# A planned decode kernel: nine transposing matmuls for sixteen, one projection for four batches, and new orders

## The chip, the cores and the metric

The kernel runs on one core of one Trainium2 chip. The metric is the device time of one execution in microseconds, the median of several runs. TensorE is PE in the profile (PEld its weight loads), VectorE DVE, ScalarE ACT, GpSimd POOL, and SyncE SP.

## The reference

Two layers of decoding for four batches, one token each, a model width D of 512. A layer is attention over a cache (32 query heads in 8 groups, 4096 keys, 128 elements a head) and a gated unit with 1792 hidden elements. Both layers use the same weights and the same cache.

```python
B, Sq, D = 4, 1, 512
Hq, Hkv, Sk, Dh = 32, 8, 4096, 128

def _A_ref(x, k_cache, v_cache, wq, wo):
    q = (x @ wq)                                   # per head, (B, Hq, 1, Dh)
    scores = einsum("bhqd,bhkd->bhqk", q, k) * (Dh ** -0.5)   # k, v repeated 4 times
    p = softmax(scores)
    o = einsum("bhqk,bhkd->bhqd", p, v)
    return o.reshape(B, Sq, Hq * Dh) @ wo

def _B_ref(x, w_gate, w_up, w_down):
    return (sigmoid(x @ w_gate) * (x @ w_up)) @ w_down

x = x + _A_ref(layernorm(x), K, V, wq, wo)
x = x + _B_ref(layernorm(x), w_gate, w_up, w_down)
x = x + _A_ref(layernorm(x), K, V, wq, wo)
x = x + _B_ref(layernorm(x), w_gate, w_up, w_down)
```

All inputs are bfloat16. K and V of one batch and one key-value head are 1 MB each.

## The kernel before

The work is cut into 64 units (layer, batch, key-value head), taken two at a time as 32 pairs. ORDER names the pairs: `013` is layer 0, batch 1, heads 6 and 7. Layer 1 of a batch can begin only when all four pairs of its layer 0, and then the gated unit and the new queries of that batch, are done, so pairs of both layers and of several batches are mixed.

K and V come from HBM into 12 slots of 1 MB; late in the kernel the four parts of the query weights' place become slots too. KEPT names the K and V that stay in their slot from layer 0 to layer 1; all others are loaded twice. LOADS is the order of all loads, one letter each (`k`, `v`, and `o`, `g`, `u`, `d` for the weights). One queue, SP's, issues them in that order. The function `pump` issues the next load as soon as a slot is free; the wait for the slot's last reader is a wait of SP, and everything behind it in LOADS waits too.

PROGRAM is the order of all steps, one letter each, in groups that begin where a pair's scores do. Each engine gets its share of the steps in this order and goes through them without overtaking. The letters, with the engine and the line that carries the work:

| letter | step | engine, line |
|---|---|---|
| `t`, `T` | half, or the whole, of a K tile transposed in 32 x 32 blocks | DVE L984 |
| `b` | the pair's query blocks | POOL L725 |
| `s`, `z` | first and second half of the pair's scores; `z` frees K slots | PE L1001 |
| `m`, `p`, `n` | row maxima, spread over the rows, made a bias | DVE L1019, PE L1024, DVE L1033 |
| `e` | Exp, with its sums | ACT L1044 |
| `P` | Exp transposed into the bank PT | PE L1063 |
| `C`, `D` | two halves of PT copied out as bfloat16, four copies each | ACT L1115 |
| `h`, `r`, `i` | sums split in two parts, summed per head, inverted | POOL L1074, PE L1129, DVE L1141 |
| `a` | half of one unit's product with V (PV); four to a pair, the second and fourth free a V slot | PE L1161 |
| `o` | `normalise`: the product times the inverted sums, into oT | DVE L1200 |
| `w`, `W` | `do_wo`: an out projection of units that are ready, added to x | PE L1219, DVE L1235 |
| `.` | one of 17 steps of a batch's gated unit and new queries | mostly PE L803, L828, L874, L923 |
| `x` | row sums of the out weights for the last unit | ACT L587 |

The buffer oT has two columns per head. Column 0 holds what is projected alone; column 1 holds a layer-1 result of batches 0 to 2 (`held`), which waits for a mate of another batch with the same unit, so that two columns go through the weights at once. `W` projects even where a mate would still come; a held result that is in the way of the next is flushed alone in `normalise`. A group for a pair of units is 32 matmuls.

After the last PV, `mean_of_last` (line 615) brings the mean of the last layernorm forward: it takes the last projection's part in it straight from oT. Then come layernorm, gated unit and the store for all four batches at once, with nothing left to load.

## Time and profile before

| | |
|---|---|
| median of 3 runs | 314.98 us (314.69 to 315.49) |
| the profiled execution | 316.39 us |
| its span, first to last instruction | 314.6 us |
| read from HBM | 119.80 MB |
| PE, DVE, ACT, POOL busy | 70%, 56%, 33%, 13% |
| PE matmuls, weight loads | 4826 each |

The page divides the span into 40 equal slices with one digit each for the busy share of an engine, the clock granted to PE and the DMA engines. Groups of instructions are by line; behind the bar stands the idle time of the engine before them and what ended it. In a timeline, the columns are start, duration, engine, line, operation, tiles, shapes, count, and in brackets the idle time before. A row of stretches has the busy time of each engine with its instructions, then the granted clock, the DMA share and the rate.

### The profile page before, as it was taken

What the parts mean: (1) busy time and instruction counts of PE and PEld (TensorE: products, weight loads), DVE (VectorE), ACT (ScalarE), POOL (GpSimd) and SP (SyncE); (2) the same over time, 40 slices, a digit from 0 to 9 for tenths busy, and PEclk for the clock granted to TensorE, in tenths of its full rate; (3) what the DMA queues carried; (4) which work ended last, traced back from release to release, by engine and by line L of the source; (5) the groups of instructions that cost most, each with busy time, mean ns of one, the idle gap of its engine ahead of it and who ended that gap; (6) DMA issues with size and microseconds to landing.
All of it is one profiled execution on the core that took longest, in us unless ns stands there. A gap on an engine that the chain in (4) does not pass through costs nothing.

```text
span 314.6 us, 11202 instructions
## 1 busy us (share of the span) xinstructions
PE 221.0 (70%) x4826; PEld 144.6 (46%) x4826; DVE 176.3 (56%) x410; ACT 104.8 (33%) x347; POOL 40.6 (13%) x205
## 2 busy tenths in 40 slices
PE   1233345327778768878988789877747888699796
PEld 1220223124555344647455646345543743455685
DVE  6266666324325657385951477865664797932243
ACT  2000322103303555342244534334333302366420
POOL 0011111100001203021021211021011110231000
PEclk9999999999985555565565557565555576555555
DMA  7999999999999999999999999999999899999900
GB/s 296 421 409 405 425 405 411 373 413 418 399 421 419 409 405 351 425 418 405 415 362 364 421 382 422 418 421 416 423 416 388 343 397 397 422 423 419 410 35 5
DMA packets 20792, 120.52 MB, mean 383 GB/s; under 512 B 1924, under 2 KB 6024, under 8 KB 7688
## 3 DMA queue, kind: packets, MB, share of 16 engines
q1 hardware_dynamic: 20720, 119.81, 94.3%
q8 instruction: 38, 0.62, 0.8%
q14 instruction: 10, 0.08, 0.1%
q10 hardware_dynamic: 24, 0.01, 0.0%
HBM read 119.80 MB, written 0.00 MB: 381 GB/s over the span
## 4 chain that ended last, share of the span: by engine, by line
PE 28%; DMA 13%; DVE 11%; ACT 6%; issue 5%; POOL 2%; DVEq 0%; ACTq 0%; POOLq 0%; SPq 0%
PE O_ps L1161 9%; PE S_ps L1001 9%; DVE slot L984 8%; DMA slot<-in_A_k_cache_dram 7%; DMA slot<-in_A_v_cache_dram 6%; ACT pT L1115 5%; PE PT L1063 2%; PE O_ps L1219 2%; POOL qz L725 1%; ACT pe L1044 1%; PE M_ps L923 1%; PE M_ps L874 1%; DVE small L1019 1%; PE S_ps L1443 1%; PE M_ps L738 1%
## 5 line engine op out<-in xcount | busy, mean ns | idle before, releaser
L984 DVE STREAM_TRANSPOSE slot<-slot 128x2048 f32<-128x2048 f32 (+1 forms) x53 | 103.9, 1973 | 17.4 <-DMA slot<-in_A_k_cache_dram 17.2
L1115 ACT ACTIVATE pT<-PT 32x128 bf16<-32x128 f32 x236 | 63.3, 268 | 90.7 <-PE PT L1063 64.3
L1001 PE MATMUL S_ps<-slot,qz 128*16 128x512 bf16 x512 | 60.4, 598 | 21.0 <-DVE slot L984 8.6
L1161 PE MATMUL O_ps<-pT,slot 128*128 128x4 bf16 x1696 | 54.2, 166 | 27.9 <-DMA slot<-in_A_v_cache_dram 18.2
L1161 PEld LDWEIGHTS O_ps<-pT,slot 128*128 128x128 bf16 x1696 | 50.8, 104 | 45.3 <-issue 15.9
L725 POOL COPY qz<-qs 32x32 bf16<-32x32 bf16 x128 | 26.1, 204 | 107.6 <-PE S_ps L1001 54.0
L1019 DVE TENSOR_REDUCE small<-S_ps 128x1 bf16<-128x512 f32 x32 | 21.9, 685 | 29.5 <-PE S_ps L1001 29.3
L1044 ACT ACTIVATE pe<-S_ps,small 128x512 bf16<-128x512 f32 x32 | 22.0, 687 | 44.4 <-DVE small L1033 34.9
L1001 PEld LDWEIGHTS S_ps<-slot,qz 128*16 128x16 bf16 x512 | 10.6, 101 | 36.6 <-issue 10.8
L1219 PE MATMUL O_ps<-oT,wo 128*128 128x2 bf16 (+1 forms) x672 | 21.6, 165 | 5.7 <-issue 3.9
L1219 PEld LDWEIGHTS O_ps<-oT,wo 128*128 128x128 bf16 x672 | 19.8, 104 | 9.2 <-issue 4.9
L1063 PE MATMUL PT<-ident_bf,pe 128*64 128x32 bf16 x512 | 19.2, 215 | 2.9 <-ACT pe L1044 2.0
L1063 PEld LDWEIGHTS PT<-ident_bf,pe 128*64 128x64 bf16 x512 | 15.8, 150 | 9.9 <-ACT pe L1044 4.9
L1074 POOL CAST small<-small 128x1 bf16<-128x1 f32 x32 | 6.0, 188 | 100.1 <-ACT pe L1044 80.9
L1200 DVE TENSOR_TENSOR oT<-O_ps,small 128x8 bf16<-128x8 f32 (+1 forms) x32 | 5.1, 160 | 22.0 <-PE O_ps L1161 14.4
L1235 DVE TENSOR_TENSOR small<-small,O_ps 128x4 f32<-128x4 f32 x34 | 4.0, 147 | 23.3 <-PE O_ps L1219 22.1
L1033 DVE CUSTOM_DVE_ANT_0 MS<-MS,small 128x64 f32<-128x64 f32 x32 | 9.2, 288 | 11.5 <-PE MS L1024 7.0
L874 PE MATMUL M_ps<-wq,small 128*1 128x512 bf16 x128 | 14.2, 608 | 0.0
L1024 PE MATMUL MS<-valid_p,small 128*128 128x64 bf16 x32 | 7.2, 224 | 6.9 <-DVE small L1019 6.7
L889 ACT ACTIVATE t_row<-M_ps,small 128x512 bf16<-128x512 f32 x4 | 2.7, 687 | 21.4 <-PE M_ps L874 17.7
L1129 PEld LDWEIGHTS O_ps<-small 128*128 128x128 bf16 x62 | 4.4, 111 | 10.4 <-issue 5.4
L1024 PEld LDWEIGHTS MS<-valid_p,small 128*128 128x128 bf16 x32 | 3.5, 109 | 12.5 <-DVE small L1019 11.2
(117 smaller groups left out, 187.0 us busy)
## 6 DMA issues: line engine op xcount, KB each, us to landing
slot<-in_A_v_cache_dram SPq DMA_DIRECT2D x49, 1024.0 KB, 10.8
slot<-in_A_k_cache_dram SPq DMA_DIRECT2D x45, 1024.0 KB, 11.6
wq<-in_A_v_cache_dram SPq DMA_DIRECT2D x6, 1024.0 KB, 12.6
wq<-in_A_wq_dram SPq DMA_DIRECT2D x2, 2048.0 KB, 10.2
wo<-in_A_wo_dram SPq DMA_DIRECT2D x8, 512.0 KB, 18.6
wg<-in_B_w_gate_dram SPq DMA_DIRECT2D x2, 896.0 KB, 17.5
wu<-in_B_w_up_dram SPq DMA_DIRECT2D x2, 896.0 KB, 20.1
wd<-in_B_w_down_dram SPq DMA_DIRECT2D x1, 1024.0 KB, 24.0
```

Of the source, the lines that this page charges most:

```text
L725: (lambda a, ps: lambda e: e.tensor_copy(qz_sb[ps, :, :, a, :], qs_sb[b][ps, :, u * REP:(u + 2) * REP].rearrange("p t (u r) -> p u t r", r ...
L874: (lambda k, st: lambda e: e.matmul(M_ps[h][32 * st:32 * st + 1, :], lhsT=xc_bf[:, k, 0:1], rhs=wv[:, k, h, :, st, :], start=(k == 0), sto ...
L984: dve(lambda e: e.transpose(kf, kf), writes=[f"s{st}"])
L1001: (lambda t, b2, e_, c, r0, ul: lambda e: e.matmul(S_ps[p][r0:r0 + 4 * REP, :], lhsT=qz_sb[:, ul, t, :, :].rearrange("p a r -> p (a r)"), ...
L1019: dve(lambda e: e.tensor_reduce(rm_bf, S_ps[p][:, :], AX.X, ALU.max), reads=[f"S{p}"], writes=["rmb"])
L1024: lambda e: e.matmul(MS[:, 0:16 * REP], lhsT=rm_bf.broadcast_to([P, P]), rhs=valid_p[:, :], start=True, stop=True),
L1033: lambda e: e.tensor_tensor_reduce(MS[:, 128:128 + 16 * REP], MS[:, 0:16 * REP], mask_f.rearrange("p n w -> p (n w)"), rowk_f, BIG, ALU.ad ...
L1044: lambda e: e.activation(pe_sb.rearrange("p j m -> p (j m)"), S_ps[p][:, :], ACTF.Exp, bias=nm_sb, scale=exp_scale, accum_out=sm_sb,),
L1063: (lambda x1, j, a1, n: lambda e: e.matmul(PT[64 * a1:64 * a1 + 64, n:n + 32], lhsT=pe_sb[:, j, 64 * x1:64 * x1 + 64], rhs=valid_bf[:, :, ...
L1115: (lambda dst, frm: lambda e: e.activation(dst, frm, ACTF.Copy))(dst, frm),
L1161: (lambda n, x, c, j: lambda e: e.matmul(bank[:, ul * REP:(ul + 1) * REP], lhsT=vv[:, x * JG + c * 4 + j, :], rhs=pT[:, x % 2, x // 2, j, ...
L1219: (lambda c, r: lambda e: e.matmul(O_ps[p][:, 64 + 2 * c:64 + 2 * c + nb], lhsT=wo_sb[:, us[0] * REP + r, cols(c)], rhs=oT_sb[:, us[0] * R ...
```

## The change

ORDER, LOADS and PROGRAM are replaced, with KEPT as it was. `ptrans` takes nine matmuls in place of 16: the four parts of the Exp tile are seen as one row of 512 columns, and a weight of 128 of them is taken every 64 columns, so that neighbours overlap; seven matmuls have 128 columns of weights and 64 result columns each, the two at the ends 64 and 32. `copies` and the PV read the new places. oT has one column per batch; in layer 1 a unit is projected once, when all four batches have their result there, with four columns. `held`, `mate_comes` and `W` are gone, `mean_of_last` has one set of eight matmuls for four columns, and x gets one addition per projection.

```diff
 
 KEPT = ["012345/23", "0145/45", "167/067", "014567/7"]
 ORDER = """
-003 002 000 001 013 011 101 010 012 100 102 022 021 020 023 112 110 031 103 111 123 032 030 033 120
-113 121 131 122 133 132 130
+000 003 002 001 013 011 101 010 012 102 100 021 022 020 023 112 110 111 031 113 123 030 032 033 120
+103 121 122 131 133 130 132
 """
 LOADS = """
-kkkkokovvk kkokvvkvoo kooovkvgvu guddvvvkkv kkvvkkvvvv kkvvkkvkvk vvvvvvkkvk kvvvkkvvkk vvkkvvkkvv
-kvvkkkvkkk vkkvvvvvvv vvvvv
+kkookkkook kovvokvvvo vokkvkkvgg uuddvvvkkv kkvvkkvvvv kkvvvkkvkk vvvvvvkkvk kvvvkkvvkk vvkkvvkkvv
+kvvkkkvkvk kkkvvvvvvv vvvvv
 """
 PROGRAM = """
-szmptntTeb shzPmDrpneTChiaawbT sazmbpTaTPonrD sTzCmpiaenahTbaaroiPDeC sazaaTamhPWprbnoiCTa
-sDaePzWhamawpoDnW.eC.rhP..iWr......aa.W..aaoi..CaDa.t.twbt szmtpnaebax
-shPzmrpCboiaDanaePThaoriCTDWWaax szWabmapntx sezPmhpWCrbtonx szDTiwbe
-szahamaPaopmCDrnWiaa.ap.enTahor..WPbT..ehiD szCaaa.aom..btWWrP.tipT..nDC.aaeT
-szh..PmawapnrCoe.iTWhDb.P saazbrmaaopn sizCaebw szmDhaaaPpornDCiehWaaamPapnrCoiDaeTWbaTwaahoPr.C
-szmDi.paaW.ne..bhTT.PaaWr s.zomC.pnib.a.Daa.eaTPT....DC sohrizm.aa.aabp snehztrmPCDoipnbeatTaP
-saazCohrimpDbnaaaTaePhDtoriCtaa szampnaoweTPhWribCaTDa szmaapnoePTWDbhri
-szCamWapnaeahPoCbritDWta.Ta..TW. sz..amab.pT.o.n s.zWmw.T.e...PChprni..aDbTawe szbTTmhPrwaaoC
-spznDiaeamPhpbrwaneaowi sCzhDbraaPm saapDzonCmweiPhpnCab
-saaaezrDoiPmhrpaaaanCeoDiWahaaaoPrCDiwaaNawWa
+szmpneTtthPrTib szDmptnetCb sazaaaPomCDbphTwwrnT seiaazPawhmbpranoDiCaehaPttaTa
+sroiwCawzDmpaTanebaTo shwPD.z.mr..pi.w.CneP...hr.aa...waaoi..CaDa..bTw swztmtpnebahaox
+sPCzmriwDpnTaebhaaaPorwiCTaDax szaawmpbwnx sztmtePbpx shDzrCwwnobetitwmaah
+spnzPawamoCrDpeihwa.a.ntaaPeD..Cbt.T.roiP szaam.haar.poi.C.anDaT.w.e.w.Thrb.aao szmPDTp.bnCeiwh.PaTa
+szambap szneroDmwpCb szniaahPrbameaowiCDharPapwanaCDoiTewaahTaaoP.ri szDmC.apban.wTe.T..hPraaoD
+s.iz.C.abm.a.panaTe.o.hPr.wTC. siD.za.amwpwaabwn soezthrmtpiPwnDCbeaaT
+shPaaCzmropinTaDeahaaPboCriDaTaw szmapneaTPChwoDriTbwaa szaampbnoTePhwrDi
+szCabmawwpnweaahPoritwtCa.DaT.T.. sz..maa.boTp.. s.zm.nbwT....pePhrtCnDi.aeat. shzPTraaTmCb
+sopnizDeawbmaPhwapwaonCDr szibemaaphnPC srzembaaD
+soiwPphCneaaraDawwoziwaPaamDaohrpiwCanaeaaPoChDwariaaNwa
 """
 
 
...
     t_row = sbt([P, D], dt.float32, "t_row")
     qs_sb = [sbt([P, NT4, HQ], dt.bfloat16, f"qs{b}") for b in range(Bn)]
     qz_sb = sbt([P, 2, NT4, 4, REP], dt.bfloat16, "qz")
-    oT_sb = sbt([P, HQ, 2], dt.bfloat16, "oT")
+    oT_sb = sbt([P, HQ, Bn], dt.bfloat16, "oT")
     pe_sb = sbt([P, 4, P], dt.bfloat16, "pe")
-    pT_sb = sbt([P, 2, 2, 4, 4, REP], dt.bfloat16, "pT")
-    NSMALL = 128
+    pT_sb = sbt([P, 2, 4, 2, 4, REP], dt.bfloat16, "pT")
+    NSMALL = 112
     small_sb = sbt([P, NSMALL], dt.float32, "small")
     used = [0]
 
...
             writes=["M1"],
         )
 
-    def mean_of_last(us, batches):
+    def mean_of_last(us):
         u = seq[NU - 1][2]
         assert us == [u]
-        cb = [(c, bb) for c, bb in enumerate(batches) if bb is not None]
         S.last_write["M1"] = S.group(
             "pe",
             [
-                (lambda n, r, c, bb, at_end: lambda e: e.matmul(
-                    M_ps[1][:, bb:bb + 1], lhsT=ws_hl[:, n, r:r + 1].broadcast_to([P, P]),
-                    rhs=oT_sb[:, u * REP + r, c:c + 1], start=False, stop=at_end,
-                ))(n, r, c, bb, (n, r, c) == (1, REP - 1, cb[-1][0]))
-                for c, bb in cb for n in range(2) for r in range(REP)
+                (lambda n, r: lambda e: e.matmul(
+                    M_ps[1][:, 0:Bn], lhsT=ws_hl[:, n, r:r + 1].broadcast_to([P, P]),
+                    rhs=oT_sb[:, u * REP + r, 0:Bn], start=False, stop=(n == 1 and r == REP - 1),
+                ))(n, r)
+                for n in range(2) for r in range(REP)
             ],
-            reads=["wsb"] + [f"oT_{u}_{c}" for c, _ in cb],
+            reads=["wsb"] + [f"oT_{u}_{c}" for c in range(Bn)],
         )
 
     def square_sums_of_parts():
...
 
     def ptrans(g):
         fns = []
-        for x1 in range(2):
-            for j in range(4):
-                for a1 in range(2):
-                    n = 32 * (4 * x1 + j)
-                    fns.append(
-                        (lambda x1, j, a1, n: lambda e: e.matmul(
-                            PT[64 * a1:64 * a1 + 64, n:n + 32],
-                            lhsT=pe_sb[:, j, 64 * x1:64 * x1 + 64],
-                            rhs=valid_bf[:, :, 8 * a1:8 * a1 + 8].rearrange("p g (a h) -> p a g h", a=2),
-                            start=True,
-                            stop=True,
-                        ))(x1, j, a1, n)
-                    )
+        pe_flat = pe_sb.rearrange("p j m -> p (j m)")
+        for q0, q1, c0, m0, m1 in (
+            [(64, P, 0, 0, 64)]
+            + [(0, P, 64 * w + 32, 64 * w, 64 * w + P) for w in range(7)]
+            + [(0, 64, 480, 448, 512)]
+        ):
+            a0, a1 = q0 // 32, q1 // 32
+            fns.append(
+                (lambda q0, q1, c0, m0, m1, a0, a1: lambda e: e.matmul(
+                    PT[q0:q1, c0:c0 + 16 * (a1 - a0)],
+                    lhsT=pe_flat[:, m0:m1],
+                    rhs=valid_bf[:, :, 4 * a0:4 * a1].rearrange("p g (a h) -> p a g h", h=REP),
+                    start=True,
+                    stop=True,
+                ))(q0, q1, c0, m0, m1, a0, a1)
+            )
         S.group("pe", fns, reads=["pe0"] + IDENT, writes=["PT"])
 
     def split_sums(g):
...
         n = buffer_of[g]
         if n == 0:
             return pT_sb, "pT0"
-        return slot[spare[0]][:, 0:16 * 4 * REP].rearrange("p (x y j g r) -> p x y j g r", x=2, y=2, j=4, g=4), "pT1"
+        return slot[spare[0]][:, 0:16 * 4 * REP].rearrange("p (x j y g r) -> p x j y g r", x=2, j=4, y=2, g=4), "pT1"
 
     def copies(g, x0):
         late = g == NP - 1
...
         for a in range(4):
             a1, a0 = divmod(a, 2)
             q = 64 * a1 + 32 * x0
-            dst = pT[32 * a:32 * a + 32, x0, :, :, :, :].rearrange("p x j g h -> p (x j) (g h)")
-            frm = PT[q:q + 32, 0:256].rearrange("p (n a w) -> p n a w", a=2, w=16)[:, :, a0, :]
+            dst = pT[32 * a:32 * a + 32, x0, :, :, :, :].rearrange("p j x g h -> p (j x) (g h)")
+            frm = PT[q:q + 32, :].rearrange("p (n a w) -> p n a w", a=4, w=16)[:, :, 2 * (1 - a1) + a0, :]
             if late and a1:
                 S.inst(
                     "dve",
...
                         (lambda n, x, c, j: lambda e: e.matmul(
                             bank[:, ul * REP:(ul + 1) * REP],
                             lhsT=vv[:, x * JG + c * 4 + j, :],
-                            rhs=pT[:, x % 2, x // 2, j, 2 * ul + c, :],
+                            rhs=pT[:, x % 2, j, x // 2, 2 * ul + c, :],
                             start=(n == 0 and c == 0 and j == 0),
                             stop=(n == XJ - 1 and c == 1 and j == 3),
                         ))(n, x, c, j)
...
         if part != 0 and (l == 1 or not kept("v", i)):
             free.append(where.pop(("v", b, u)))
 
-    held = {}
     ready = []
     done = set()
+    own_column = max((i, b) for i, (l, b, _) in enumerate(seq) if l == 0)[1]
 
     def normalise(g, uls=(0, 1)):
         l, b, u = seq[2 * g]
         bank, key = out_of(g, uls[0])
-        c = 1 if l == 1 and b < Bn - 1 else 0
+        c = b if l == 1 else own_column
         u0, n = u + uls[0], len(uls)
-        old = sorted({held[u + ul] for ul in uls if c and u + ul in held})
-        for bb in old:
-            us = [u + ul for ul in uls if held.get(u + ul) == bb]
-            for x in us:
-                held.pop(x)
-            wo_units(us, (None, bb), (g + 1) % 2)
         for ul in uls:
-            assert c or not any(t[2] == u + ul for t in ready)
+            assert not any(t[0] == l and t[2] == u + ul for t in ready)
             done.add((l, b, u + ul))
-            if c:
-                held[u + ul] = b
-            else:
+            if l == 0 or all((1, bb, u + ul) in done for bb in range(Bn)):
                 ready.append((l, b, u + ul))
         dve(
             lambda e: e.tensor_tensor(
...
             writes=[f"oT_{u + ul}_{c}" for ul in uls],
         )
 
-    def wo_units(us, batches, p, then=None):
-        c0 = 0 if batches[0] is not None else 1
-        cs = [c for c in range(2) if batches[c] is not None]
-        nb = len(cs)
+    def wo_units(us, l, b, p, then=None):
+        bs = range(Bn) if l == 1 else [b]
+        cs = range(Bn) if l == 1 else [own_column]
+        nb = len(bs)
         n = REP * len(us)
+        out_w = O_ps[p][:, 64:64 + KD * nb]
         fns = []
         for c in range(KD):
             for r in range(n):
                 fns.append(
                     (lambda c, r: lambda e: e.matmul(
-                        O_ps[p][:, 64 + 2 * c:64 + 2 * c + nb],
+                        out_w[:, c * nb:(c + 1) * nb],
                         lhsT=wo_sb[:, us[0] * REP + r, cols(c)],
-                        rhs=oT_sb[:, us[0] * REP + r, c0:c0 + nb],
+                        rhs=oT_sb[:, us[0] * REP + r, cs[0]:cs[0] + nb],
                         start=(r == 0),
                         stop=(r == n - 1),
                     ))(c, r)
...
             "pe", fns, reads=[f"oT_{u}_{c}" for u in us for c in cs] + [f"wo{u}" for u in us], writes=[f"O{p}"]
         )
         if then is not None:
-            then(us, batches)
-        for n_, c in enumerate(cs):
-            bb = batches[c]
-            dve(
-                (lambda n_, bb: lambda e: e.tensor_tensor(
-                    xT[:, :, bb],
-                    xT[:, :, bb],
-                    O_ps[p][:, 64:64 + 2 * KD].rearrange("p (k two) -> p k two", two=2)[:, :, n_],
-                    ALU.add,
-                ))(n_, bb),
-                reads=[f"x{bb}", f"O{p}"],
-                writes=[f"x{bb}"],
-            )
-
-    def mate_comes(t):
-        l, b, u = t
-        if u in held:
+            then(us)
+        dve(
+            lambda e: e.tensor_tensor(
+                xT[:, :, bs[0]:bs[0] + nb],
+                xT[:, :, bs[0]:bs[0] + nb],
+                out_w.rearrange("p (k b) -> p k b", k=KD),
+                ALU.add,
+            ),
+            reads=[f"O{p}"],
+            writes=[f"x{bb}" for bb in bs],
+        )
+
+    def do_wo(p, then=None):
+        if not ready:
             return False
-        end = 2 * last[l, b] if l == 0 else NU - 1
-        return any(pos[1, b2, u] <= end + 1 and (1, b2, u) not in done for b2 in range(Bn - 1))
-
-    def do_wo(p, force=False, then=None):
-        todo = [t for t in ready if force or not mate_comes(t)]
-        if not todo:
-            return False
-        l, b, u = todo[0]
+        l, b, u = ready.pop(0)
         us = [u]
-        if (l, b, u + 1) in todo and u % 2 == 0:
+        if u % 2 == 0 and (l, b, u + 1) in ready:
+            ready.remove((l, b, u + 1))
             us.append(u + 1)
-        for x in us:
-            ready.remove((l, b, x))
-        mates = {held.get(x) for x in us}
-        if len(mates) == 1 and None not in mates:
-            for x in us:
-                held.pop(x)
-            wo_units(us, (b, mates.pop()), p, then)
-        else:
-            wo_units(us, (b, None), p, then)
+        wo_units(us, l, b, p, then)
         return True
 
     ln_a(0, Bn, RS)
...
             k_turn(i)
         elif c == "x":
             wo_row_sums(sums_left.pop(0))
-        elif c in "wW":
-            do_wo((count["o"] + 1) % 2, c == "W")
+        elif c == "w":
+            do_wo((count["o"] + 1) % 2)
         elif c == ".":
             b, f = passes.pop(0)
             assert count["o"] > last[0, b] and not any(t[:2] == (0, b) for t in ready)
...
     assert all(count[c] == n for c, n in dict(D=NP, r=NP, i=NP, o=NP - 1, N=1, a=4 * NP).items())
     g = NP - 1
     xkeys = [f"x{b}" for b in range(Bn)]
-    while do_wo((g + 1) % 2, True):
+    while do_wo((g + 1) % 2):
         pass
     parts(sq_hl, xT.rearrange("p k b -> p (k b)"), xkeys, "rb")
     mean_before()
     normalise(g, (1,))
-    do_wo((g + 1) % 2, True, mean_of_last)
-    assert not ready and not held
+    do_wo((g + 1) % 2, mean_of_last)
+    assert not ready
     free += spare
     assert not loads and len(free) == NSLOT + KD
 
```

## The prediction

> **What bounds the kernel now.** I read the page first (totals, slices, the chain that ended last), then the answer by stretches, then the queue that issues the loads, and last the final microseconds one instruction at a time.
>
> ```profile
> span 314.6 us, 11202 instructions
> ...
> PE 221.0 (70%) x4826; PEld 144.6 (46%) x4826; DVE 176.3 (56%) x410; ACT 104.8 (33%) x347; POOL 40.6 (13%) x205
> ...
> PEclk9999999999985555565565557565555576555555
> DMA  7999999999999999999999999999999899999900
> GB/s 296 421 409 405 425 405 411 373 413 418 399 421 419 409 405 351 425 418 405 415 362 364 421 382 422 418 421 416 423 416 388 343 397 397 422 423 419 410 35 5
> ...
> HBM read 119.80 MB, written 0.00 MB: 381 GB/s over the span
> ...
> PE 28%; DMA 13%; DVE 11%; ACT 6%; issue 5%; POOL 2%; DVEq 0%; ACTq 0%; POOLq 0%; SPq 0%
> ...
> slot<-in_A_v_cache_dram SPq DMA_DIRECT2D x49, 1024.0 KB, 10.8
> ```
>
> The DMA row is full from the second slice to slice 38, and empty in the last two. At the 416 GB/s of an ordinary stretch (128 to 160 us in the next fence) the 119.80 MB take 288 us; the last two slices, in which nothing is left to load, are another 15 us. So about 12 us of the span are neither. The engines are not the bound by their totals (PE 70%), yet the chain puts 28% on PE and 13% on DMA: loads and compute hand over to each other, because a load may start only when a step of the program has given a slot back. The stretches tell where that hand-over fails:
>
> ```profile
> core 0: us, PE busy (x) PEld busy (x) DVE busy (x) ACT busy (x) POOL busy (x), PEclk, DMA share, GB/s
> ...
> 104.00:128.00 24.00, 18.58 (x362) 10.60 (x362) 15.41 (x30) 12.34 (x40) 5.19 (x26) 0.50 0.99 390
> 128.00:160.00 32.00, 26.97 (x606) 18.48 (x600) 22.26 (x54) 13.18 (x43) 4.47 (x22) 0.61 1.01 416
> 160.00:172.00 12.00, 11.33 (x238) 6.44 (x235) 2.64 (x12) 3.51 (x13) 2.02 (x10) 0.50 0.93 342
> ...
> 240.00:268.00 28.00, 23.75 (x437) 14.25 (x437) 21.53 (x50) 8.33 (x27) 3.25 (x16) 0.61 0.97 378
> ...
> 300.00:314.60 14.60, 11.07 (x368) 10.17 (x365) 6.13 (x36) 2.12 (x8) 0.00 (x0) 0.50 0.02 6
> ```
>
> Against 416 GB/s, 104 to 128 lacks 24 x 26/416 = 1.5 us of transfer, 160 to 172 lacks 12 x 74/416 = 2.1 us, and 240 to 268 lacks 28 x 38/416 = 2.6 us: 6.2 us in all. That is the most that new orders can win back inside the loads. The queue shows what a failing hand-over looks like:
>
> ```profile
> 103.87 1.99 SPq L366 DMA_DIRECT2D slot<-in_A_v_cache_dram  x2
> 110.31 1.81 SPq L366 DMA_DIRECT2D slot<-in_A_k_cache_dram  x2
> ...
> 151.70 14.84 SPq L366 DMA_DIRECT2D slot<-in_A_v_cache_dram  x6
> 166.59 3.14 SPq L366 DMA_DIRECT2D slot<-in_A_k_cache_dram  x2
> ```
>
> A load of 1024 KB takes 1.049 MB / 416 GB/s = 2.5 us of transfer. Between the end of the issues at 105.86 and the next at 110.31 lie 4.45 us, the time of 1.8 loads; and six V loads take from 151.70 to 166.54, 14.8 us where their transfer takes 15.1, so no reserve builds up ahead of 166. The order of the steps on PE decides there.
>
> **The change, part by part.** First the loads. I counted LOADS, ORDER, KEPT and NSLOT: 115 slot and weight loads after the query weights, the same sizes, the same number kept. So the transfer time stays. I then walked both PROGRAM strings and wrote down for every load which step frees its slot, with the PE work ahead of that step. From load 38 (counted from 0) on, 75 of the 77 positions wait for the same kind of step of the same pair; ahead of them stands the same PE work within 0.9 us, apart from one that is 2.1 us earlier. The big difference is the head: pair 000 comes first, and five output-weight loads stand before its second V load, where two stood. That load goes from 12.6 MB into the queue to 16.2 MB, so the first PV is some 9 us later at the 400 GB/s of the early slices. I cost it at nothing: twelve slots are free at the start, PE stands at one to five tenths in the first eight slices, and from byte 35.9 MB on both queues hold the same kind of load. If that cover were gone, up to 9 us of the first PV's delay would show as missing transfer before 100 us.
>
> The Exp transposition, `P` in the program, drops 7 of 16 matmuls in each of 32 pairs.
>
> ```profile
> 32.38 0.61 PE L1063 MATMUL PT<-ident_bf,pe 128*64 128x32 bf16 x16
> ...
> 190.53 0.43 PE L1063 MATMUL PT<-ident_bf,pe 128*64 128x32 bf16 x16
> ...
> 294.17 0.99 PE L1161 MATMUL O_ps<-pT,wq 128*128 128x4 bf16 x32
> ...
> 298.47 1.85 PE L1161 MATMUL O_ps<-slot,slot 128*128 128x4 bf16 x64
> ```
>
> ```profile
> L1063 PE MATMUL PT<-ident_bf,pe 128*64 128x32 bf16 x512 | 19.2, 215 | 2.9 <-ACT pe L1044 2.0 <-ACT pT L1115 0.8
> ...
> L1024 PE MATMUL MS<-valid_p,small 128*128 128x64 bf16 x32 | 7.2, 224 | 6.9 <-DVE small L1019 6.7
> ...
> L1129 PE MATMUL O_ps<-small 128*128 128x8 bf16 x62 | 6.4, 174 | 3.1 <-POOL small L1077 1.4 <-DVE small L1235 0.9 <-PE MS L1024 0.8
> ```
>
> A group of 16 with a matmul of 215 ns at its end in 0.61 us has starts (610 - 215)/15 = 26 ns apart, for 32 columns each. If a matmul had a price of its own, nine would cost nine of the PV's: 64 of those take 1.85 us against 0.99 for 32, so 27 ns each, and the new group would be 8 x 27 + 224 = 0.44 us. If the price goes by columns, nothing is won: 16 x 32 = 512 columns before, 7 x 64 + 2 x 32 = 512 after. The rows nearest to that question are the single matmuls of 64 and of 8 columns, 224 and 174 ns: 50 ns for 56 columns, 0.9 ns a column, which makes 29 ns for 32 columns, close to the 26 seen, and 57 for 64. By columns the group is 7 x 57 + 29 + 215 = 0.64 us. I take that the group stays near 0.61, a gain of 0; the bounds are 0.44 and 0.64. The lower one would take 32 x 0.17 = 5.4 us off PE; at PE's 28% of the chain 1.5 us of the span.
>
> [...]
>
> The copies behind it read blocks of 16 elements at a stride of 64 in place of 32, with the same shape; they are costed at nothing more.
>
> The gathered projection:
>
> ```profile
> L1219 PE MATMUL O_ps<-oT,wo 128*128 128x2 bf16 (+1 forms) x672 | 21.6, 165 | 5.7 <-issue 3.9 <-DVE oT L1200 1.9
> ...
> L1235 DVE TENSOR_TENSOR small<-small,O_ps 128x4 f32<-128x4 f32 x34 | 4.0, 147 | 23.3 <-PE O_ps L1219 22.1 <-PE MS L1024 1.2
> ```
>
> I count 16 groups of 32 matmuls in the first layer both times; in the second, five times 32 become four times, because no product has to be flushed alone. 32 matmuls at 27 ns are 0.86 us of PE. The group that vanishes stands in `normalise` of pair 123, so every freeing step from the PV of pair 22 on (load 92) has 0.9 us less PE work ahead. Between 240 and 268 us PE is busy 23.75 of 28 us and the loads lack 2.6 us, so part of it counts: I take half, 0.4; bounds 0 and 0.9. Four result columns in place of one or two cost nothing: the same 27 ns hold for the PV's four. On DVE 34 additions of 147 ns become 21: 1.9 us, off the path, since DVE is 56% busy. Waits: the layer-2 projections of a unit now wait for all four batches, but they are put in the program where the fourth is done, and only the end of the kernel reads them.
>
> The orders, in the stretch 160 to 172:
>
> ```profile
> 160.17 1.03 PE L1001 MATMUL S_ps<-slot,qz 128*16 128x512 bf16 x8
> ...
> 161.13 1.01 PE L1161 MATMUL O_ps<-pT,slot 128*128 128x4 bf16 x32
> ```
>
> Before, PE has `P` of pair 13, then `s` of pair 14, then the PV `a` of pair 12 that frees the slot that load 63, a V, waits for ("Db.P saaz" in PROGRAM). After, it is `P`, the PV, then `s` ("PaTa szam"): the slot comes free 161.13 - 160.17 = 0.96 us sooner, in the stretch that lacks 2.1 us. I count 1.0 us; bounds 0 and 2.1. Of POOL's and SP's own steps nothing else moves past a wait: qz's copies (`b`) stand one pair ahead as before.
>
> The tail:
>
> ```profile
> 304.85 0.56 PE L1219 MATMUL O_ps<-oT,wo 128*128 128x2 bf16 x16
> ...
> 305.27 0.56 PE L615 MATMUL M_ps<-oT,small 128*128 128x1 bf16 x16
> 305.52 0.23 DVE L1235 TENSOR_TENSOR small<-small,O_ps 128x4 f32<-128x4 f32 x2 [0.89 <-PE O_ps L1219]
> ...
> 305.95 0.17 DVE L501 SCALAR_TENSOR_TENSOR t_row<-M_ps,small 128x16 f32<-128x16 f32 x1
> ```
>
> mean_of_last has 8 matmuls in place of 16, and the next DVE step (305.95) waits for the last of them: 8 x 27 = 0.2 us off the end. The addition at 305.52 lies beside them.
>
> ```profile
> q8 instruction: 38, 0.62, 0.8%
> ...
> 297.84 0.69 PEld L1219 LDWEIGHTS O_ps<-oT,wo 128*128 128x128 bf16 x23 [1.18 <-issue]
> ```
>
> PE has 528 instructions fewer of 9652 (2 x 224, 2 x 32, 2 x 8), so about two of 38 instruction fetches. One wait without a releaser, 1.18 us, stands in the tail; which instruction it hits after cannot be told. I take 0, bounds a microsecond either way.
>
> Sum: 0 (transposition) - 0.4 (projection) - 1.0 (orders) - 0.2 (tail) = -1.6 us, so a span of 313.0. The profiled execution took 316.39 us, 1.8 more than its span, and is 1.4 above the median of 314.98; moved by the same amount, the median becomes **313.4 us**.
>
> **The rivals.** *Slower: freeing steps that stand later.* In the stretch from 104 to 128, pair 6's first PV frees the slot of the K load issued at 110.31, with the queue 1.8 loads short. Before, the program has "iaDana" there; after, "iwDpnTaebha", in which `w`, a projection of 32 matmuls, stands ahead of it: 0.9 us later on PE. Load 61, a V, waits for the PV of pair 11 in place of scores, 0.8 us later by the same count of PE work (a score group of 0.96 less, PVs at 27 ns more). If the queue is dry at both, and the gain at 160 us is eaten, this gives +0.9 + 0.8 - 0.2 = +1.5, so **316.5**. It decides once fewer than two loads are outstanding when that K load is issued. For it: 390 GB/s there. Against: the next freeing steps of pair 7 have the same PE work ahead in both programs, so a late load may be overtaken by a queue that is full again.
>
> *No change:* loads set the pace, each saving ends in a wait for the next one, and only the tail's 0.2 us is seen: **314.8**. For it: the DMA row; against: 6.2 us of missing transfer.
>
> *The transposition does gain:* price for each matmul, -1.6 - 1.5 = -3.1: **311.9**. The 0.43 us at 190.53 is against it: with the same 16 matmuls the time fell, so the number of instructions is no floor.
>
> *That the change doesn't do what it says* is excluded for the bytes and the counts, which I took from the strings.
>
> **How the numbers follow.** About 0.3% (0.94 us) is what a measurement of this kernel can tell from no change. The forecast gets 0.44, the cheap transposition 0.06: faster 0.50. No change 0.22. The late frees 0.28, because three microseconds of PE order decide, and a rearranged program can lose at places that the trace of before doesn't show. Range: downwards from 311.9 by the rest of the 160 to 172 stretch (1.1) to 310.8; upwards from 316.5 by half a microsecond of fetch luck to 317.0. The likeliest case alone (the sum with half its bounds) is 312.3 to 314.2.
>
> **What would show it.** Right: `P` groups of 9 matmuls at 0.60 to 0.64 us; more than 342 GB/s around 160 to 172; transfer ending 1 us or more sooner; still about 14 us from there to the end, 0.2 less. Wrong: `P` groups near 0.44 us (the transposition pays); under 390 GB/s between 104 and 128 with an issue gap of over 4.45 us before pair 6's K load (late frees); or a hole before 100 us (the head was no cover).

## The result, and the profile after

The changed kernel takes **313.68 us** (median of 22 runs), the kernel before 314.87 us in the same comparison: a ratio of 0.9963 [0.9945, 0.9981], 0.37% faster. The forecast was 313.4 us. Ratios compare runs on the same chip and leave disturbed runs out, so they are not to the last digit the quotients of the medians. The profiled execution of the changed kernel took 316.34 us and is one of its long ones, as the 316.39 us of before was; a second profile of the same kernel, taken in the experiments (e5), took 313.81 us with a span of 312.0. Where the two differ, both are given.

The page of the kernel after, with the totals, the two rows of the transfer, the instruction queue, the chain, and the group of the new transposition:

```profile
span 314.5 us, 10670 instructions
...
PE 227.9 (72%) x4562; PEld 146.8 (47%) x4562; DVE 176.3 (56%) x399; ACT 104.5 (33%) x347; POOL 40.4 (13%) x205
...
DMA  7999999999999999999999999999999998999910
GB/s 294 419 397 394 410 404 409 402 420 420 400 416 419 373 394 420 424 418 418 420 391 390 417 349 424 425 419 418 418 418 387 412 373 315 380 426 423 414 51 5
...
q8 instruction: 36, 0.59, 0.7%
...
PE 36%; DMA 34%; DVE 10%; SPq 9%; ACT 6%; issue 4%; POOL 1%; DVEq 0%; ACTq 0%; POOLq 0%
...
L1065 PE MATMUL PT<-ident_bf,pe 128*128 128x64 bf16 (+1 forms) x288 | 27.7, 236 | 7.8 <-ACT pe L1043 7.2 <-ACT pT L1117 0.5
```

PE has 264 matmuls fewer and is busy for 6.9 us *more* (227.9 against 221.0). The last line says where: the transposition's 288 matmuls occupy 27.7 us where the 512 of before occupied 19.2. Bytes are as counted, and so are the packets of the queue `q8`, named "instruction", which the prediction called instruction fetches: 36 in place of 38. The shares of the chain changed (PE 28 to 36%, DMA 13 to 34%), though the total hardly did: the chain names whichever of two nearly equal ones came last at each hand-over.

The same answer by stretches as in the prediction, of the kernel after:

```profile
core 0: us, PE busy (x) PEld busy (x) DVE busy (x) ACT busy (x) POOL busy (x), PEclk, DMA share, GB/s
...
0.00:68.00 68.00, 24.56 (x486) 16.06 (x486) 33.75 (x65) 14.16 (x47) 5.98 (x33) 1.00 1.00 393
104.00:128.00 24.00, 20.91 (x386) 11.91 (x379) 16.44 (x34) 12.21 (x40) 5.57 (x28) 0.98 0.99 397
...
160.00:172.00 12.00, 11.48 (x226) 6.71 (x223) 3.21 (x11) 4.13 (x15) 3.15 (x16) 0.50 0.98 379
240.00:268.00 28.00, 23.32 (x373) 13.05 (x365) 19.91 (x42) 6.50 (x21) 3.66 (x18) 0.58 0.91 365
300.00:314.50 14.50, 9.12 (x313) 8.48 (x311) 5.33 (x31) 1.58 (x6) 0.00 (x0) 0.50 0.04 12
```

From 160 to 172 us the rate rose from 342 to 379 GB/s: 12 x 37/416 = 1.07 us of transfer, the 1.0 that the orders were credited with. Between 240 and 268 it fell from 378 to 365: 28 x 13/416 = 0.9 us given back. From 104 to 128 it went from 390 to 397. The second profile (e5) has the same signs and other sizes:

```profile
160.00:172.00 12.00, 11.48 (x226) 6.72 (x223) 3.21 (x11) 4.68 (x17) 3.19 (x16) 0.50 1.00 405
240.00:268.00 28.00, 24.11 (x421) 14.09 (x417) 22.27 (x48) 8.19 (x26) 4.00 (x20) 0.62 0.96 374
```

Here 1.8 us are won at 160 to 172 and 0.3 us are given back at 240 to 268.

The queue that issues the loads, around pair 6's K load:

```profile
105.07 1.85 SPq L366 DMA_DIRECT2D slot<-in_A_v_cache_dram  x2
111.70 1.18 SPq L366 DMA_DIRECT2D slot<-in_A_k_cache_dram  x2
```

The gap ahead of that load is 111.70 - 106.92 = 4.78 us, longer than the 4.45 of before, as the slower rival had it, but the rate of the stretch did not fall.

PE of the kernel after, one line for each group: pair 13's transposition and what follows, and the tail from the last transposition on.

```profile
158.58 0.89 PE L1065 MATMUL PT<-ident_bf,pe 128*64 128x32 bf16 x9 [0.84 <-ACT pe L1043]
159.82 1.01 PE L1163 MATMUL O_ps<-pT,slot 128*128 128x4 bf16 x32 [0.35 <-DMA slot<-in_A_v_cache_dram]
160.76 1.89 PE L1000 MATMUL S_ps<-slot,qz 128*16 128x512 bf16 x16
...
298.49 0.89 PE L1065 MATMUL PT<-ident_bf,pe 128*64 128x32 bf16 x9
299.31 0.72 PE L1214 MATMUL O_ps<-oT,wo 128*128 128x4 bf16 x21
301.88 0.46 PE L1214 MATMUL O_ps<-oT,wo 128*128 128x4 bf16 x11 [1.85 <-issue]
...
305.51 0.35 PE L614 MATMUL M_ps<-oT,small 128*128 128x4 bf16 x8
```

The PV that frees load 63's slot now stands ahead of the scores and starts at 159.82 in place of 161.13. Of the 32 transpositions 29 take 0.88 to 0.89 us (the other three 0.65 to 0.72), not the 0.61 of before and not the 0.60 to 0.64 forecast. In the tail mean_of_last takes 0.35 us (0.56 before). A wait of 1.85 us without a releaser stands in the last projection; before, its counterpart of 1.18 us ended at 297.84, 3.1 us ahead of the landing of the last load (300.98); here the wait ends at 301.88, and the last load lands at 302.16.

The starts of the single matmuls, from the trace, explain the 0.89 us. Counted in ns from the PV matmul ahead of the group (left of the bar), through the group, to the first matmul behind it (right of the bar), for a group with nothing to wait for:

```
before, 16 x 64 wide   0 | 96 100 172 174 227 227 280 280 334 334 387 387 440 440 494 494 | 640
after,  64, 7 x 128, 64  0 | 96 261 307 359 413 466 519 573 744 | 913
```

The 16 of before do not start 26 ns apart: they start two at a time, 53 ns from pair to pair (76 from the first pair to the second). The two of a pair write the two 64-row halves of PT (`PT[64 * a1:64 * a1 + 64]`), and start 0 to 4 ns apart. The nine of after start some 53 ns apart as well, except where the width of the weights changes: 165 ns from the 64-wide first to the 128-wide second, 171 to the 64-wide last, and 169 from that to the 128-wide matmul behind the group. Each of these three changes of width costs about 115 ns more than the 53 of a step; the fourth, from the 128-wide PV into the group, shows as 96 ns (e4 below has 26 there). Between 128-wide neighbours, a group of before has two changes (at its two edges), one of after four.

### The profile page after: what moved, and what is told of

Same layout as the page of the kernel before. It is cut to its first block, busy times and chain, and to the rows that moved or that the text cites. A ratio compares the mean times of both kernels' runs of the same rounds, so it can differ in the third digit from the quotient of the medians.

```text
span 314.5 us, 10670 instructions
## 1 busy us (share of the span) xinstructions
PE 227.9 (72%) x4562; PEld 146.8 (47%) x4562; DVE 176.3 (56%) x399; ACT 104.5 (33%) x347; POOL 40.4 (13%) x205
## 4 chain that ended last, share of the span: by engine, by line
PE 36%; DMA 34%; DVE 10%; SPq 9%; ACT 6%; issue 4%; POOL 1%; DVEq 0%; ACTq 0%; POOLq 0%
DMA slot<-in_A_v_cache_dram 17%; DMA slot<-in_A_k_cache_dram 13%; PE O_ps L1163 10%; PE S_ps L1000 10%; SPq L366 7%; DVE slot L983 6%; PE PT L1065 4%; DMA wq<-in_A_v_cache_dram 4%; ACT pT L1117 4%; PE O_ps L1214 3%; PE M_ps L873 2%; PE M_ps L922 1%; DVE small L1018 1%; ACT pe L1043 1%; SPq L346 1%
## 5 line engine op out<-in xcount | busy, mean ns | idle before, releaser
L1000 PE MATMUL S_ps<-slot,qz 128*16 128x512 bf16 x512 | 59.5, 586 | 25.4 <-DVE slot L983 13.2
L1065 PE MATMUL PT<-ident_bf,pe 128*128 128x64 bf16 (+1 forms) x288 | 27.7, 236 | 7.8 <-ACT pe L1043 7.2
L1065 PEld LDWEIGHTS PT<-ident_bf,pe 128*128 128x128 bf16 (+1 forms) x288 | 20.4, 124 | 21.6 <-ACT pe L1043 11.4
L1214 PE MATMUL O_ps<-oT,wo 128*128 128x1 bf16 (+1 forms) x640 | 20.3, 165 | 3.7 <-issue 1.8
L1214 PEld LDWEIGHTS O_ps<-oT,wo 128*128 128x128 bf16 x640 | 18.7, 104 | 6.1 <-issue 2.8
L1228 DVE TENSOR_TENSOR small<-small,O_ps 128x4 f32<-128x4 f32 (+1 forms) x21 | 3.1, 150 | 13.1 <-PE O_ps L1214 12.9
L827 PE MATMUL M_ps<-wu,small 128*1 128x512 bf16 (+1 forms) x64 | 8.7, 543 | 0.0
```

The source lines that it names most:

```text
L1000: (lambda t, b2, e_, c, r0, ul: lambda e: e.matmul(S_ps[p][r0:r0 + 4 * REP, :], lhsT=qz_sb[:, ul, t, :, :].rearrange("p a r -> p (a r)"), ...
L1065: (lambda q0, q1, c0, m0, m1, a0, a1: lambda e: e.matmul(PT[q0:q1, c0:c0 + 16 * (a1 - a0)], lhsT=pe_flat[:, m0:m1], rhs=valid_bf[:, :, 4 * ...
L1214: (lambda c, r: lambda e: e.matmul(out_w[:, c * nb:(c + 1) * nb], lhsT=wo_sb[:, us[0] * REP + r, cols(c)], rhs=oT_sb[:, us[0] * REP + r, c ...
```

## The experiments

In each, "ratio" is to the kernel before, with its 95% interval. The first four take the change apart: the transposition alone in or out, the projection alone, and the transposition without changes of width.

**e1_after_with_16** is the kernel after with the 16 matmuls of before in `ptrans` (and its strides in the copies):

```diff
-                    PT[q0:q1, c0:c0 + 16 * (a1 - a0)],
-                    lhsT=pe_flat[:, m0:m1],
...
+        for x1 in range(2):
+            for j in range(4):
+                for a1 in range(2):
...
+                            PT[64 * a1:64 * a1 + 64, n:n + 32],
+                            lhsT=pe_sb[:, j, 64 * x1:64 * x1 + 64],
```

> The changed kernel with the transposition by 16 matmuls put back (with the places of PT, the copies and the PV that belong to it); orders and gathered projection stay. In the trace of the changed kernel a transposition group takes 0.89 us, not the 0.61 of before: a gap of some 170 ns stands after the first and ahead of the last of the nine, where the matmul is 64 wide and its neighbour 128. That is 32 x 0.28 = 9 us more of PE. Theory A, PE's order counts and the transposition loses: 1 to 2.5 us faster than the changed kernel (about 311.5), the whole gain comes from orders and projection. Theory B, the loads set the pace and hide the longer groups: within 0.5 us of the changed kernel. Theory C, the transposition is what gains, by fewer instructions: slower than the changed kernel by 1 us, about the time of before.

Measured: 314.96 us, ratio 0.9994 [0.9966, 1.0023]. This is the run that holds the prediction's three gains (orders, projection, tail) and nothing else. They were forecast to be worth 1.6 us together, a ratio of 0.995; that lies outside the interval. The time is that of "no change".

**e2_before_with_9** is the kernel before with the nine matmuls, the same edit the other way round:

```diff
-                            PT[64 * a1:64 * a1 + 64, n:n + 32],
-                            lhsT=pe_sb[:, j, 64 * x1:64 * x1 + 64],
...
+                    PT[q0:q1, c0:c0 + 16 * (a1 - a0)],
+                    lhsT=pe_flat[:, m0:m1],
```

> The kernel before with the transposition by nine matmuls alone; its orders and its projection stay. Theory A: groups of 0.89 us, about 2.5 us slower than before (28% of 9 us), 317.4. Theory B: within 0.5 us of before. Theory C: faster than before by about 1 us.

Measured: 318.96 us, 1.0125 [1.0088, 1.0162]. In the old orders the kernel with the nine matmuls is slower by 0.9 to 1.6%; how much of that is the longer group is taken up with e10 and e11.

**e3_before_orders_gathered** is the kernel before, with its own orders and 16 matmuls, and the layer-2 projection gathered for four batches:

```diff
-        c = 1 if l == 1 and b < Bn - 1 else 0
+        c = b if l == 1 else own_column
...
-            if c:
-                held[u + ul] = b
-            else:
+            if l == 0 or all((1, bb, u + ul) in done for bb in range(Bn)):
```

> The kernel before with the gathered projection alone: its ORDER, LOADS, PROGRAM and 16 matmuls stay, and a W is taken as a w. Against e1 it differs in the orders only. Theory that the orders bring the gain (1.0 of the predicted 1.6): 0.2 to 0.6 us faster than before, and e1 clearly faster than this. Theory that the projection and the shorter end bring it: 1 us or more faster than before, and e1 no faster than this.

Measured: 314.81 us, 0.9996 [0.9967, 1.0025]. Gathering, with the eight matmuls of `mean_of_last` that come with it, moves nothing that can be measured; the 0.4 and 0.2 us taken for the two (0.2% together) are within the interval, as is zero.

**e4_full_width_ends** is the kernel after, with the first and the last matmul also 128 wide. The 64 weight columns that they lack are taken from constants that now lie on either side of `pe` in the same tile; the rows of PT that these produce are overwritten or never read.

```diff
+    row_of_pe = sbt([P, P + 4 * P + 64], dt.bfloat16, "pe")
+    ident_bf = row_of_pe[:, 0:P]
+    valid_p = row_of_pe[:, 5 * P:5 * P + 16 * REP]
-            [(64, P, 0, 0, 64)]
+            [(64, P, 0, -64, 64)]
...
-                    PT[q0:q1, c0:c0 + 16 * (a1 - a0)],
-                    lhsT=pe_flat[:, m0:m1],
+                    PT[:, c0:c0 + 16 * (a1 - a0)],
+                    lhsT=row_of_pe[:, P + m0:P + m0 + P],
```

> The changed kernel with all nine matmuls 128 wide: the two at the ends take 64 more weight columns from constants beside the Exp tile, whose results land where nobody reads. If the gaps of 170 ns come from the change of width between 64 and 128, the group falls from 0.89 to about 0.66 us (7 x 53 + 2 x 27 + 240 ns); if they come from something else at the ends (32 columns in place of 64, the first weight load), it stays near 0.89. With 0.66, theory A says 1 to 2 us faster than the changed kernel, theory B no difference.

Measured: 313.27 us, 0.9926 [0.99, 0.9951]. Its group in the list by line, and one group of its tail in the timeline of PE:

```profile
L1065 PE MATMUL PT<-pe 128*128 128x64 bf16 (+1 forms) x288 | 18.9, 228 | 7.6 <-ACT pe L1044 6.9 <-ACT pT L1117 0.6
```

```profile
296.71 0.59 PE L1065 MATMUL PT<-pe 128*128 128x32 bf16 x9
```

27.7 us became 18.9, and 0.89 became 0.59 (0.66 was expected), with the same nine matmuls, the same columns and the same orders. The starts, counted as above, are

```
full width, 9 x 128    0 | 26 53 82 132 185 239 292 345 399 | 452
```

so the waits at the edges are gone too, in front of the group (26 in place of 96 ns) and behind it (53 in place of 169). From 26 to 452 are 426 ns for 512 columns, 0.83 ns a column: the price by columns of the prediction, once no width changes. This is the shown cause of the long group: the change of weight width, not the price of a matmul and not that of a column. From the matmul ahead to the one behind, a pair costs PE 640 ns before, 913 after and 452 with full width; over 32 pairs that is up to 8.7 us more and up to 6.0 us less than before.

The second four ask whether the orders carry the gain, and whether the place of the code does.

**e5_after_again** is the kernel after, with no edit.

> The changed kernel as it is, beside the next three on one chip. All theories: 0.9945 to 0.9981 of before again. If it comes out at e1's 0.999 the gain of 1.2 us was within what one chip differs from another; if at 0.996, the 16 matmuls of e1 cost something that the group's length does not show.

Measured: 313.9 us, 0.9974 [0.9949, 0.9998]; with a span of 312.0 in its profile.

**e6_full_width_shifted** and **e7_16_shifted** are e4 and e1 with 32 idle matmuls of four columns in PE's stream while it waits for its first loads (6.19 us up to 13.74 us in before), which moves all that follows 64 instructions (32 weight loads, 32 matmuls) down the stream:

```diff
+    S.group(
+        "pe",
+        [lambda e: e.matmul(O_ps[1][:, 0:4], lhsT=ident_bf[:, :], rhs=ident_bf[:, 0:4], start=True, stop=True)] * 32,
+        reads=IDENT,
+        writes=["O1"],
+    )
```

> e4 (nine matmuls of full width) with 32 more matmuls of four columns ahead of everything, in the time in which PE waits for the query weights: some 0.9 us of PE that nothing waits for, but every later instruction of PE stands 64 further in its stream. In every trace so far a wait of PE without a releaser (1.2 to 2.5 us) stands in the last 15 us, after a number of PE instructions that is 66 or 67 above a multiple of 128. Theory P, the place of these fetches in the stream decides up to a microsecond or two: the wait moves to other steps and the time differs from e4's by 0.5 us or more, either way. Theory N, the fetches cost the same wherever they fall: e4's time within 0.4 us.

> e1 (changed kernel, 16 matmuls) with the same 32 extra matmuls at the start. Theory P: e1's loss against the changed kernel is the place of its fetches (two waits of 0.9 and 2.1 us between 291 and 298 us); shifted by half their distance it comes out 1 us or more faster, 0.992 to 0.996 of before. Theory N, or the number of instructions counts: still 0.998 to 1.001.

Measured: e6 314.5 us, 0.9978 [0.996, 0.9996]; e7 314.71 us, 0.9987 [0.9966, 1.0009]. Full width lost half a per cent by being moved (0.9926 to 0.9978); for the 16 no difference can be told (0.9994 to 0.9987).

**e8_scores_before_pv** is the kernel after with the one swap on which the forecast put 1.0 us undone: pair 14's first scores ahead of pair 12's PV again (and the transposition `T` of a K tile ahead of both).

```diff
-spnzPawamoCrDpeihwa.a.ntaaPeD..Cbt.T.roiP szaam.haar.poi.C.anDaT.w.e.w.Thrb.aao szmPDTp.bnCeiwh.PaTa
-szambap szneroDmwpCb szniaahPrbameaowiCDharPapwanaCDoiTewaahTaaoP.ri szDmC.apban.wTe.T..hPraaoD
+spnzPawamoCrDpeihwa.a.ntaaPeD..Cbt.T.roiP szaam.haar.poi.C.anDaT.w.e.w.Thrb.aao szmPDTp.bnCeiwh.PT
+saazambap szneroDmwpCb szniaahPrbameaowiCDharPapwanaCDoiTewaahTaaoP.ri szDmC.apban.wTe.T..hPraaoD
```

> The changed kernel with the step put back on which the prediction's order term rests: pair 14's first scores stand ahead of pair 12's first PV (with the transposition of their K ahead of both). Prediction: the slot of load 63 comes free about 1 us later, the stretch from 160 to 172 falls from 379 GB/s towards 342, and the kernel is 0.5 to 1 us slower than the changed kernel. Rival: the loads catch up later, and the time is that of the changed kernel within 0.3 us.

Measured: 314.83 us, 0.9984 [0.9956, 1.0012]. By stretches:

```profile
160.00:172.00 12.00, 11.48 (x229) 6.69 (x222) 3.22 (x11) 4.20 (x15) 3.19 (x16) 0.50 0.93 345
```

The rate of the stretch fell back to 345 GB/s, as it was before the change (342), from the 379 of after (405 in e5's profile). So the mechanism is the one forecast: order of these two steps, time of the slot, rate of the stretch. What the kernel lost by it can't be told: 0.1% against e5 (0.9974), timed beside it, 0.2% against the first comparison (0.9963), each with an uncertainty of some 0.3 to 0.4%, so that neither nothing nor the forecast's 0.3% is excluded. The rates suggest that part of what is won at 165 us is given back later.

The last four take the place of the code and the width to the orders of before.

**e9_before_shifted** is the kernel before with the 32 idle matmuls, **e10_before_9_shifted** is e2 with them (the edit of e6 in both):

```diff
+        [lambda e: e.matmul(O_ps[1][:, 0:4], lhsT=ident_bf[:, :], rhs=ident_bf[:, 0:4], start=True, stop=True)] * 32,
```

> The kernel before with the 32 extra matmuls of e6 ahead of everything (64 PE instructions, in time that PE has free). Theory P: the place of the fetches is worth as much here as between e4 and e6 (0.5%), so the time differs from before by 0.2 to 0.6% either way; if it is faster by 0.3%, the whole gain of the change is no more than such a shift gives. Theory N: before within 0.15%.

> e2 (before with nine matmuls, 1.25% slower than before) with the 32 extra matmuls. Theory A, the longer groups stand in the way in before's orders: still 1.0 to 1.4% slower. Theory P, e2's loss is an unlucky place of its fetches: at most 0.6% slower.

Measured: e9 319.86 us, 1.011 [1.0057, 1.0164]; e10 317.88 us, 1.0078 [1.0053, 1.0103]. The kernel before loses 1.1% by work put where PE is idle anyway. PE's timeline of e9 (an execution of 321.0 us) shows how:

```profile
183.51 0.40 PE L1069 MATMUL PT<-ident_bf,pe 128*64 128x32 bf16 x7 [2.99 <-issue]
...
193.73 0.56 PE L1167 MATMUL O_ps<-pT,slot 128*128 128x4 bf16 x16 [1.55 <-issue]
...
200.89 0.64 PE L1167 MATMUL O_ps<-pT,slot 128*128 128x4 bf16 x19 [1.40 <-issue]
```

Three waits that nothing releases, 2.99, 1.55 and 1.40 us, fall within 18 us; before had one of 1.30 us in this stretch, at 198.92. The V loads that a step behind them frees are issued 5 us later (first fence: before; second: e9), and the rate from 204 to 216 falls from 421 to 322 GB/s (third: before; fourth: e9):

```profile
205.04 0.80 SPq L366 DMA_DIRECT2D slot<-in_A_v_cache_dram  x2
```

```profile
210.13 0.80 SPq L366 DMA_DIRECT2D slot<-in_A_v_cache_dram  x2
```

```profile
204.00:216.00 12.00, 8.55 (x198) 5.17 (x195) 7.41 (x15) 4.63 (x16) 2.39 (x12) 0.64 1.01 421
```

```profile
204.00:216.00 12.00, 9.79 (x166) 4.34 (x158) 7.97 (x13) 4.31 (x14) 2.00 (x10) 0.50 0.82 322
```

These waits come at fixed places of PE's stream. Before has such waits too; the longest of its five stands between 104 and 128 us:

```profile
115.32 0.19 PE L1219 MATMUL O_ps<-oT,wo 128*128 128x2 bf16 x2 [2.31 <-issue]
```

In all fourteen traces, every wait of PE of over 0.45 us in which neither the matmul nor its weight load waits for a semaphore, 52 in all and two to six in each, stands at an instruction whose number is 192 or 193 modulo 256, when weight loads, matmuls and the semaphore and drain instructions of PE's queue are counted together from 0 (with the weight loads and matmuls alone, no common remainder appears). Their lengths go from about 0.5 to 3 us. The instruction queue `q8` moves packets of 16,384 bytes, 36 of them for the 9272 instructions of after, one for 258. And each of the 52 waits ends 1.26 to 1.62 us after such a packet has ended. From the traces:

| run | PE waits, us | remainder | the packet before ended, us | from there to the end of the wait |
|---|---|---|---|---|
| before | 113.01 to 115.32 | 192 | 113.96 | 1.36 |
| after | 300.03 to 301.88 | 193 | 300.60 | 1.28 |
| e9 | 180.53 to 183.51 | 193 | 181.99 | 1.52 |
| e9 | 192.18 to 193.73 | 193 | 192.34 | 1.39 |
| e9 | 199.48 to 200.89 | 192 | 199.52 | 1.37 |

From this the author takes it that PE waits there for its own instructions; no run changed a packet of that queue alone, so it is a reading of these numbers. The 32 idle matmuls move each of these places by 64 instructions, a quarter of the way to the next, and not by half, as e7's expectation had it.

e10 lies between its two theories. Moved, the nine matmuls come out 0.5% lower (1.0125 to 1.0078, just outside the uncertainty), and no slower than the 16 moved likewise (1.011, e9). So e2's 1.25% isn't the price of the longer groups alone; the place of the code has a part in it.

**e11_before_9_full_width** is e2 with e4's edit, and **e12_full_width_again** is e4 once more, with no further edit.

```diff
-            [(64, P, 0, 0, 64)]
+            [(64, P, 0, -64, 64)]
```

> e2 with all nine matmuls 128 wide, so that a transposition group takes 0.59 us as in e4, in before's orders; the number of PE instructions is e2's. Theory A: the loss of e2 goes, 0.995 to 1.002 of before. If the loss stays at 1.0% or more, the length of the group has nothing to do with it.

> e4 again, beside the others: the fastest kernel so far (0.990 to 0.995 of before). If 0.0068 to 0.0080 below before again, it beats the changed kernel (0.9963 and 0.9974) for certain; if it comes out at 0.996, e4 was a lucky sample and full width is worth nothing that can be told.

Measured: e11 314.23 us, 0.9956 [0.9928, 0.9983]; e12 312.74 us, 0.9933 [0.9902, 0.9963]. In the orders of before, taking the width changes out turns a loss of 1.25% into a gain of 0.44%; e2 and e11 have the same number of PE instructions, so the place of the code is the same in both. In the orders of after, again at the same place, it is worth about 0.4% (0.9926 and 0.9933 against 0.9963 and 0.9974; the intervals overlap a little). All ratios together:

| | 16 matmuls | nine, ends 64 wide | nine, all 128 wide |
|---|---|---|---|
| PE per pair, edges included | 640 ns | 913 ns | 452 ns |
| orders of before | 1 | 1.0125 | 0.9956 |
| the same, 64 instructions later | 1.011 | 1.0078 | not run |
| orders of after, gathered | 0.9994 | 0.9963, 0.9974 | 0.9926, 0.9933 |
| the same, 64 instructions later | 0.9987 | not run | 0.9978 |

The fastest version is the last column of the third row, 313.27 and 312.74 us: ahead of the kernel before for certain, ahead of the changed kernel by 0.4% in two runs, and no longer ahead of it once it is moved by 64 instructions (0.9978).

## Why the prediction was right, and where it was not

The total came out (313.68 us against 313.4; 0.37% or 1.2 us faster, where 1.6 were forecast), and that is luck. The sum behind it did not: its three gains, run by themselves (e1), give nothing that can be measured; the term put at 0 adds more work to PE than the three take off; and what makes up the difference isn't settled.

**The transposition: mis-sized, 0.89 us against 0.61 to 0.64.** The step that failed is "starts (610 - 215)/15 = 26 ns apart". It is a mean over a group whose starts are 0, 4, 76, 78, 131 ns and so on, and the mean hid that the 64-wide matmuls start two at a time. The 26 ns that the prediction saw in it are half of a pair's 53. The price by columns is right for 128-wide matmuls all the same: 53 ns for 64 columns, where 57 were put. What it left out is that the new group mixes widths; the four changes in each pair weigh more than all that was argued about. Both bounds, 0.44 and 0.64, were too low, since none of the rows behind them had a change of width in it. With the width held, the group takes 0.59 us, and two changes at its edges vanish that before had: up to 6.0 us of PE off before's sum. At PE's 28% of the chain that is 1.7 us. Measured by the ratios, e1 to e4 and e12 is 2.1 and 1.9 us, and before to e11 is 1.4; the moved pair, e7 to e6, shows 0.3 with an uncertainty of 0.9, less than that. In each of these pairs the place of the code differs as well. The rival's numbers (5.4 us of PE, 1.5 us of time) thus come near those of a kernel that this change nearly is, but by chance: its price for each matmul isn't what brings them, the edges are.

**Orders, -1.0: the place right, the worth not shown.** The swap acts where the forecast said, on the slot that it said, by 1.07 us of transfer against 1.0 (1.8 in e5's profile). e8 finds 0.1 to 0.2% for it and can tell that neither from nothing nor from the forecast's 0.3%. That the time in one stretch is not lost again in a later one was assumed, not read.

**Projection, -0.4, and tail, -0.2.** e3 finds 0.04%, with 0.3% of uncertainty, so the 0.4 us is neither shown nor excluded. From the start of the last transposition to the end, before takes 314.60 - 300.25 = 14.35 us, after 314.50 - 298.49 = 16.01, of which 1.85 is the wait; with all of it taken off 14.16, the 0.2 less that was forecast (e5 has 15.48 and a wait of 1.30, so 14.18; how much of the wait reaches the end was not tried). Counted from the landing of the last load, as the prediction's sign had it, it is 13.6 us before, 12.4 after and 12.0 in e5: over a microsecond less, not 0.2. The prediction took the end of the transfer for the start of a fixed tail. But the last PV begins 2.7 us behind that landing before, 1.9 after and 1.5 in e5, with no wait of PE just ahead of it: PE was late there, and how late differs from profile to profile.

**Instruction fetches: put at 0, a microsecond either way.** Too narrow: the same work 64 instructions later costs before 1.1%, about 3.5 us, and full width 0.5%. The single waits are up to 3 us long, not 1.18, and the trace of before had five over 0.45 us, 6.2 us together, where the prediction counted one.

**The head** was rightly costed at nothing: 393 GB/s over the first 68 us (394 before), and no hole in the transfer.

**The rivals.** The late free of pair 6's K load did come (4.78 us of gap), but the queue held out, and the rate rose to 397 (394 in e5). The end of the transfer, forecast a microsecond sooner, shows it in one profile only: the last load has landed at 302.16 us in after and at 300.05 in e5, against 300.98 before. "No change" is what e1 shows for the new orders with the old transposition.

**What stays open** is where the 0.37% comes from. Adding the nine matmuls to the orders of after (e1 to after) made the kernel no slower, although PE has up to 8.7 us more to do, while the same step in the orders of before cost 1.25%, though nothing that can be told where both kernels are moved (e9 to e10). The candidates are that the new orders leave more room around a transposition, and that with 448 PE instructions fewer other steps stand at the places of the waits without a semaphore; e9 shows that the second alone can be worth 1.1%. The two were not separated: any change to the number of instructions moves what stands at those places too. A hint, from one profile each, speaks for the second: these waits of over 0.45 us add up to 6.2 us in e1, and to 2.7 and 4.7 us in the two profiles of the changed kernel. For the same reason the kernel before is itself one draw among several, and a difference of 0.3% between two orders can't be put down to the orders.

## What to carry to other kernels

Before costing a group by its mean spacing, look at the single starts: the mean of 26 ns showed here neither that pairs start 0 to 7 ns apart nor that a change of weight width takes 165 to 172 ns, as in the new group. Count the changes of width, at the edges of a group too, and keep one width even at the price of multiplying columns that nobody reads (0.89 us became 0.59 by it here). And before a few tenths of a per cent are put down to an order, time the same program moved by a few idle instructions: here that alone was worth up to 1.1%.

## What the runs showed of the hardware

- In the groups of 0.89 us (after), a change between 64 and 128 weight columns takes PE 165 to 172 ns from start to start, where equal widths take 53; into a 64-wide group from 128-wide matmuls of four columns it takes 96 in place of the 26 of e4.
- In the groups of 0.61 us of before, the two 64-wide matmuls that write the two halves of PT start 0 to 7 ns apart, and from pair to pair it is 53 ns for 32 columns each. A 128-wide matmul of 64 columns takes the same 53 ns in the groups of 0.89 us (after) and 0.59 us (e4).
- PE's waits of over 0.45 us without a semaphore, up to 3 us long, 52 in fourteen traces, all come at the numbers 192 or 193 of every 256 instructions of its stream, and end 1.26 to 1.62 us after a packet of the instruction queue has ended. Moving the code by 64 instructions changed the time of one kernel by 1.1% (before to e9) and of another by 0.5% (e4 to e6).
